# Moving a kernel's input transposes from TensorE to the DMA engines, with four PSUM buffers and a bf16 weight preparation

## The chip, the cores and the metric

The kernel runs on one core of one Trainium2 chip. The metric is device time in microseconds (us). Most repetitions of one kernel agree closely; a run that lies over 1.5% above the fastest of the same kernel is labelled slow. Comparisons below use fast runs, unless a sentence says otherwise. A ratio is the mean time of one kernel's fast runs over that of the kernel before in the same rounds on the same chip, so it is not quite the ratio of the medians quoted beside it.

Names: PE is TensorE (PEld its weight loads), ACT is ScalarE, DVE is VectorE, POOL is GpSimd, SP is SyncE (here it only issues DMAs). `L209` is line 209 of the kernel in question; each kernel has its own numbering.

## The reference

A gated recurrence over time feeds a "maximum of two projections" network. Four sequences of 6144 tokens have 256 features each; the hidden width is 1024.

```python
sig = 1 / (1 + exp(-f_logit))
f = lower_bound + (1 - lower_bound) * sig
h = f[:, t] * h + (1 - f[:, t]) * x[:, t]      # for every t; y[:, t] = h
g = maximum(y @ w1, y @ w2)
out = g @ w_out
```

Both kernels use max(a, b) = a + relu(b - a), so `out = relu(y @ (w2 - w1)) @ w_out + y @ (w1 @ w_out)`. In the code `w21` is w2 - w1, `wob` is w_out, and `w13b` is w1 @ w_out, computed once at the start.

## The kernel before

Work goes in 48 blocks of 512 tokens. The recurrence wants features on partitions and time along the row, but x and f arrive with tokens on partitions, so something has to transpose them. Here TensorE does, in bf16, after DMA loads that cast from fp32.

```python
TB, TSB, NSB = 512, 128, 4
ps_t = tile_pool(name="ps_t", bufs=2, PSUM)     # transposes: 2 banks
ps_d = tile_pool(name="ps_d", bufs=2, PSUM)     # dT: 2 banks
ps_o = tile_pool(name="ps_o", bufs=1, PSUM)     # psO0..psO3: 4 banks

def recurrence(j):
    for h in range(2):                          # two halves of the features
        for i in range(NSB):
            nc.tensor.transpose(tT[:, i*TSB:(i+1)*TSB], blk.xn[:, i, h*P:(h+1)*P], ident_b)
        for i in range(NSB):
            nc.tensor.transpose(tT[:, TB+i*TSB:TB+(i+1)*TSB], blk.fn[:, i, h*P:(h+1)*P], ident_b)
        nc.scalar.activation(out=u, in_=fT, func=AF.Sigmoid, scale=-1.0)
        # DVE: ff = 1 + (lb-1)*u ; v = (1-lb)*u*xT ; y = scan(ff, v)
        # ... cut ...

def moe(j):
    for fc in range(8):
        for kc in range(2):                     # dT = (y @ w21) transposed
            nc.tensor.matmul(dT, lhsT=w21[:, kc, fc*P:(fc+1)*P], rhs=yk[kc], ...)
        nc.scalar.activation(out=rt, in_=dT, func=AF.Relu)
    for fc in range(8):                         # 32 products of 256 columns
        for i in range(NSB):
            nc.tensor.matmul(psos[i], lhsT=rts[fc][:, i*TSB:(i+1)*TSB], rhs=wob[:, fc, :], ...)
    for i in range(NSB):                        # 8 products of 256 columns
        for kc in range(2):
            nc.tensor.matmul(psos[i], lhsT=yk[kc][:, i*TSB:(i+1)*TSB], rhs=w13b[:, kc, :], ...)
    # DVE copies psO to osb, SP stores osb
```

Of the kernel before, what the change touches and what calls it, by code (L numbers as in the profile page):

```python
# [9 lines left out]
FP32 = mybir.dt.float32  # L10
BF16 = mybir.dt.bfloat16
ALU = mybir.AluOpType
# [5 lines left out]
def kernel(  # L18
# [14 lines left out]
    assert D == 2 * P and DFF == 8 * P  # L33
    KC = D // P
    FC = DFF // P
    TB = 512
    TSB = 128
    NSB = TB // TSB
    assert S % TB == 0
    NBLK_PER_B = S // TB  # L40
    NBLK = B * NBLK_PER_B

    const = ctx.enter_context(tc.tile_pool(name="const", bufs=1))
    wpool = ctx.enter_context(tc.tile_pool(name="wpool", bufs=1))
    natpool = ctx.enter_context(tc.tile_pool(name="nat", bufs=3))
    midpool = ctx.enter_context(tc.tile_pool(name="mid", bufs=2))
    ypool = ctx.enter_context(tc.tile_pool(name="ypool", bufs=4))
    rpool = ctx.enter_context(tc.tile_pool(name="rpool", bufs=10))
    opool = ctx.enter_context(tc.tile_pool(name="opool", bufs=3))
    ps_t = ctx.enter_context(tc.tile_pool(name="ps_t", bufs=2, space=bass.MemoryType.PSUM))  # L50
    ps_d = ctx.enter_context(tc.tile_pool(name="ps_d", bufs=2, space=bass.MemoryType.PSUM))
    ps_o = ctx.enter_context(tc.tile_pool(name="ps_o", bufs=1, space=bass.MemoryType.PSUM))

    ident = const.tile([P, P], FP32)
    make_identity(nc, ident[:])
# [14 lines left out]
        op1=ALU.add,  # L70
    )

    w1n = wpool.tile([P, KC, DFF], FP32)
    nc.sync.dma_start(out=w1n[:], in_=moe_w1.rearrange("(kc p) f -> p kc f", p=P))
    w2n = wpool.tile([P, KC, DFF], FP32)
    nc.sync.dma_start(out=w2n[:], in_=moe_w2.rearrange("(kc p) f -> p kc f", p=P))
    w21 = wpool.tile([P, KC, DFF], BF16)
    nc.vector.tensor_tensor(out=w21[:], in0=w2n[:], in1=w1n[:], op=ALU.subtract)

    won = wpool.tile([P, FC, D], FP32)  # L80
    nc.sync.dma_start(out=won[:], in_=moe_w_out.rearrange("(fc p) c -> p fc c", p=P))
    wob = wpool.tile([P, FC, D], BF16)
    nc.vector.tensor_copy(out=wob[:], in_=won[:])

    w1T = wpool.tile([P, FC, D], FP32)
    for kc in range(KC):
        for g in range(FC // 4):
            pt = ps_d.tile([P, TB], FP32, name="dT")
            for j in range(4):
                fc = 4 * g + j  # L90
                nc.tensor.transpose(  # L91
                    pt[:, j * P : (j + 1) * P],
                    w1n[:, kc, fc * P : (fc + 1) * P],
                    ident[:],
                )
            for j in range(4):
                fc = 4 * g + j
                nc.scalar.copy(
                    out=w1T[:, fc, kc * P : (kc + 1) * P], in_=pt[:, j * P : (j + 1) * P]
                )  # L100

    w13b = wpool.tile([P, KC, D], BF16)
    for kc in range(KC):
        psw = ps_d.tile([P, TB], FP32, name="dT")
        for fc in range(FC):
            nc.tensor.matmul(  # L106
                psw[:, 0:D],
                lhsT=w1T[:, fc, kc * P : (kc + 1) * P],
                rhs=won[:, fc, :],
                start=(fc == 0),  # L110
                stop=(fc == FC - 1),
            )
        nc.scalar.copy(out=w13b[:, kc, :], in_=psw[:, 0:D])

    class Blk:
        pass

    blocks: list = []
    for b in range(B):
        for c in range(NBLK_PER_B):  # L120
            blk = Blk()
            blk.b = b
            blk.c = c
            blk.t0 = c * TB
            blocks.append(blk)

    def out_rows(blk, i0, n):
        r0 = blk.b * S + blk.t0 + i0 * TSB
        return out[r0 : r0 + n * TSB, :].rearrange("(i p) d -> p i d", p=P)

    ys = {}

    def load_nat(blk):
        xn = natpool.tile([P, NSB, D], BF16, name="xn")
        fn = natpool.tile([P, NSB, D], BF16, name="fn")
        nc.gpsimd.dma_start(  # L136
            out=xn[:],
            in_=x[blk.b, blk.t0 : blk.t0 + TB, :].rearrange("(i p) d -> p i d", p=P),
        )
        nc.gpsimd.dma_start(  # L140
            out=fn[:],
            in_=f_logit[blk.b, blk.t0 : blk.t0 + TB, :].rearrange(
                "(i p) d -> p i d", p=P
            ),
        )
        blk.xn = xn
        blk.fn = fn

    def recurrence(j):
        blk = blocks[j]  # L150
        prev = ys.get(j - 1) if blk.c > 0 else None
        yh = []
        for h in range(KC):
            tT = ps_t.tile([P, 2 * TB], BF16, name="tT")
            xT = tT[:, 0:TB]
            fT = tT[:, TB : 2 * TB]
            for i in range(NSB):
                nc.tensor.transpose(  # L158
                    tT[:, i * TSB : (i + 1) * TSB],
                    blk.xn[:, i, h * P : (h + 1) * P],  # L160
                    ident_b[:],
                )
            for i in range(NSB):
                nc.tensor.transpose(  # L164
                    tT[:, TB + i * TSB : TB + (i + 1) * TSB],
                    blk.fn[:, i, h * P : (h + 1) * P],
                    ident_b[:],
                )
            u = midpool.tile([P, TB], BF16, name="u")
            nc.scalar.activation(out=u[:], in_=fT, func=AF.Sigmoid, scale=-1.0)  # L170
            ff = midpool.tile([P, TB], BF16, name="ff")
            nc.vector.tensor_scalar(  # L172
                out=ff[:],
                in0=u[:],
                scalar1=lbm1[:, h : h + 1],
                scalar2=1.0,
                op0=ALU.mult,
                op1=ALU.add,
            )
            v = midpool.tile([P, TB], BF16, name="v")  # L180
            nc.vector.scalar_tensor_tensor(  # L181
                out=v[:],
                in0=u[:],
                scalar=om[:, h : h + 1],
                in1=xT,
                op0=ALU.mult,
                op1=ALU.mult,
            )
            y = ypool.tile([P, TB], BF16, name=f"y{h}")
            init = 0.0 if prev is None else prev[h][:, TB - 1 : TB]  # L190
            nc.vector.tensor_tensor_scan(  # L191
                out=y[:],
                data0=ff[:],
                data1=v[:],
                initial=init,
                op0=ALU.mult,
                op1=ALU.add,
            )
            yh.append(y)
        ys[j] = tuple(yh)  # L200

    def moe(j):
        blk = blocks[j]
        yk = ys[j]
        rts = []
        for fc in range(FC):
            dT = ps_d.tile([P, TB], FP32, name="dT")
            for kc in range(KC):
                nc.tensor.matmul(  # L209
                    dT[:, :],  # L210
                    lhsT=w21[:, kc, fc * P : (fc + 1) * P],
                    rhs=yk[kc][:, :],
                    start=(kc == 0),
                    stop=(kc == KC - 1),
                )
            rt = rpool.tile([P, TB], BF16, name="rt")
            nc.scalar.activation(out=rt[:], in_=dT[:], func=AF.Relu)  # L217
            rts.append(rt)
        psos = [ps_o.tile([P, D], FP32, name=f"psO{i}") for i in range(NSB)]
        for fc in range(FC):  # L220
            for i in range(NSB):
                nc.tensor.matmul(  # L222
                    psos[i][:, :],
                    lhsT=rts[fc][:, i * TSB : (i + 1) * TSB],
                    rhs=wob[:, fc, :],
                    start=(fc == 0),
                    stop=False,
                )
        for i in range(NSB):
            for kc in range(KC):  # L230
                nc.tensor.matmul(  # L231
                    psos[i][:, :],
                    lhsT=yk[kc][:, i * TSB : (i + 1) * TSB],
                    rhs=w13b[:, kc, :],
                    start=False,
                    stop=(kc == KC - 1),
                )
        for g in range(NSB // 2):
            osb = opool.tile([P, 2, D], FP32, name="osb")
            for q in range(2):  # L240
                nc.vector.tensor_copy(out=osb[:, q, :], in_=psos[2 * g + q][:, :])  # L241
            nc.sync.dma_start(out=out_rows(blk, 2 * g, 2), in_=osb[:])

    load_nat(blocks[0])
    if NBLK > 1:
        load_nat(blocks[1])
    recurrence(0)
    for j in range(NBLK):
        if j + 2 < NBLK:
            load_nat(blocks[j + 2])  # L250
        if j + 1 < NBLK:
            recurrence(j + 1)
        moe(j)


# [28 lines left out]
```

## Time and profile before

| | before |
|---|---|
| median, 16 runs | 501.34 us |
| span of the profiled run | 498.8 us |
| first `dT` matmul of the loop | 25.25 us |
| one block in the loop | 9.79 us |
| PE work in one block | 8.7 us |

The first view is the timeline of PE: start and duration in us, engine, line, operation, output<-inputs, shape, count, and in brackets the idle time before it with what ended it. This is one block of the kernel before.

```profile
201.27 0.39 PE L158 MATMUL tT<-ident_b,xn 128*128 128x128 bf16 x4
201.50 0.39 PE L164 MATMUL tT<-ident_b,fn 128*128 128x128 bf16 x4
...
202.38 0.81 PE L209 MATMUL dT<-y,w 128*128 128x512 bf16 x3
203.59 0.59 PE L209 MATMUL dT<-y,w 128*128 128x512 bf16 x2 [0.40 <-ACT rt L217]
204.03 0.27 PE L222 MATMUL psO<-wob,rt 128*128 128x256 bf16 x1
204.13 0.59 PE L209 MATMUL dT<-y,w 128*128 128x512 bf16 x2
...
206.81 0.59 PE L209 MATMUL dT<-y,w 128*128 128x512 bf16 x2
207.24 3.11 PE L222 MATMUL psO<-wob,rt 128*128 128x256 bf16 x27
210.19 1.04 PE L231 MATMUL psO<-w13b,y 128*128 128x256 bf16 x8
211.06 0.39 PE L158 MATMUL tT<-ident_b,xn 128*128 128x128 bf16 x4
```

Read the starts, not the durations: matmuls overlap, so durations add up to more than the time passed. The sixteen transposes take 0.89 us, and 40 `psO` products take 4.35 us at 108 ns each. The `dT` phase holds sixteen matmuls of 216 ns (3.45 us) and five early `psO` products (0.54 us), yet it lasts from 202.16 to 207.24 us: 1.1 us of it is waiting. (One `dT` record per block is missing in this trace, the one at 202.16; the trace of the changed kernel lacks one too, so it shows fifteen.) ScalarE's timeline for the same block shows what PE waits for:

```profile
201.97 1.08 ACT L170 ACTIVATE u<-tT 128x512 bf16<-128x512 bf16 x2 [3.66 <-DVE osb L241]
202.94 1.09 ACT L217 ACTIVATE rt<-dT 128x512 bf16<-128x512 f32 x2
204.28 1.14 ACT L217 ACTIVATE rt<-dT 128x512 bf16<-128x512 f32 x2 [0.25 <-PE dT L209]
```

Two sigmoids come first, then eight relus. With two `dT` buffers, PE can be only two tiles ahead of the relus. The page's DMA queues (packets, MB, share of 16 engines) of the kernel before; q0 carries the casting loads, q1 the stores and weights:

```profile
q0 software_dynamic: 50688, 25.17, 40.0%
q1 hardware_dynamic: 27968, 28.32, 17.7%
```

### The profile page before, as it was taken

The numbers are of one execution on the slowest core, as the hardware profiler recorded it, in microseconds if no ns is written. First come the engines' busy times: TensorE is split into PE (matmuls) and PEld (weight loads), VectorE is DVE, ScalarE is ACT, GpSimd is POOL, SyncE is SP. The second block draws the span as 40 slices with busy tenths as digits, with TensorE's granted clock in tenths as the row PEclk, the third lists the DMA queues.
The fourth block names the chain that finished last, engine by engine and source line by source line (L and its number), as shares of the span: only waits on it lengthen the run. The fifth ranks groups of instructions, "written<-read, shape, count | busy, mean of one in ns | idle before, by whom it ended". The sixth has DMA issues, their size and how long they took to land.

```text
span 498.8 us, 8901 instructions
## 1 busy us (share of the span) xinstructions
PE 450.9 (90%) x3456; PEld 314.3 (63%) x3504; DVE 295.3 (59%) x485; ACT 269.6 (54%) x500; POOL 72.2 (14%) x102
## 2 busy tenths in 40 slices
PE   2899999999999999999999999999999989999996
PEld 1765665676567656756765676667567656766663
DVE  2466467646765675566467656756664666567451
ACT  3266546645654665466456646654664566456543
POOL 4121112111111211121111112111211111120000
PEclk9999999999999999999999999999999999999999
DMA  8947546745664575467556645754674566464112
GB/s 246 175 87 122 90 87 131 121 85 107 124 111 85 127 116 97 85 131 119 90 103 126 111 85 127 115 98 85 132 121 86 107 119 113 86 125 88 44 43 84
DMA packets 78699, 54.06 MB, mean 108 GB/s; under 512 B 3393, under 2 KB 78145, under 8 KB 78657
## 3 DMA queue, kind: packets, MB, share of 16 engines
q0 software_dynamic: 50688, 25.17, 40.0%
q1 hardware_dynamic: 27968, 28.32, 17.7%
q8 instruction: 27, 0.44, 0.3%
q14 instruction: 16, 0.12, 0.1%
HBM read 53.48 MB, written 25.17 MB: 158 GB/s over the span
## 4 chain that ended last, share of the span: by engine, by line
PE 55%; ACT 26%; DVE 9%; issue 6%; DMA 2%; ACTq 0%; POOL 0%; DVEq 0%; POOLq 0%
PE psO L222 29%; PE dT L209 22%; ACT rt L217 16%; DVE osb L241 9%; ACT u L170 9%; DMA fn<-in_f_logit_dram 2%; PE psO L231 2%; PE dT L106 1%; PE dT L91 0%; ACTq L217 0%; PE tT L164 0%; POOL xn L136 0%; PE tT L158 0%; ACTq L170 0%; DVEq L279 0%
## 5 line engine op out<-in xcount | busy, mean ns | idle before, releaser
L217 ACT ACTIVATE rt<-dT 128x512 bf16<-128x512 f32 x384 | 216.4, 601 | 36.0 <-PE dT L209 35.0
L209 PE MATMUL dT<-y,w 128*128 128x512 bf16 x720 | 202.3, 377 | 32.0 <-ACT rt L217 20.5
L222 PE MATMUL psO<-wob,rt 128*128 128x256 bf16 x1536 | 214.4, 272 | 0.0
L222 PEld LDWEIGHTS <-rt 128*128 128x128 bf16 x1536 | 149.6, 97 | 53.6
L241 DVE COPY osb<-psO 128x256 f32<-128x256 f32 x192 | 68.2, 417 | 164.3 <-PE psO L231 164.3
L170 ACT ACTIVATE u<-tT 128x512 bf16<-128x512 bf16 x96 | 52.4, 595 | 172.7 <-DVE osb L241 164.7
L209 PEld LDWEIGHTS <-w 128*128 128x128 bf16 x768 | 72.3, 97 | 107.6 <-issue 59.9
L191 DVE TENSOR_TENSOR_SCAN y<-ff,y,v 128x512 bf16<-128x512 bf16 x88 | 112.5, 1278 | 1.5
L136 POOL DMA_DIRECT2D xn<-in_x_dram x48 | 35.7, 744 | 374.2 <-PE tT L164 364.6
L181 DVE SCALAR_TENSOR_TENSOR v<-u,om,tT 128x512 bf16<-128x512 bf16 x96 | 69.4, 723 | 0.0
L172 DVE TENSOR_SCALAR ff<-u,lbm 128x512 bf16<-128x512 bf16 x96 | 46.5, 485 | 20.5 <-ACT u L170 20.5
L231 PE MATMUL psO<-w13b,y 128*128 128x256 bf16 x384 | 49.8, 273 | 0.0
L231 PEld LDWEIGHTS <-y 128*128 128x128 bf16 x384 | 37.6, 98 | 4.3
L164 PE MATMUL tT<-ident_b,fn 128*128 128x128 bf16 x384 | 37.8, 221 | 2.4 <-DMA fn<-in_f_logit_dram 2.4
L158 PE MATMUL tT<-ident_b,xn 128*128 128x128 bf16 x384 | 37.6, 221 | 2.6 <-DMA xn<-in_x_dram 2.6
L140 POOL DMA_DIRECT2D fn<-in_f_logit_dram x48 | 36.3, 756 | 1.8 <-PE dT L209 1.3
L158 PEld LDWEIGHTS <-xn 128*128 128x128 bf16 x384 | 27.7, 99 | 4.2 <-DMA xn<-in_x_dram 3.0
L164 PEld LDWEIGHTS <-fn 128*128 128x128 bf16 x384 | 25.8, 99 | 2.8 <-DMA fn<-in_f_logit_dram 2.7
L91 PE MATMUL dT<-ident,w1n 128*128 128x128 f32 x16 | 4.1, 422 | 6.6 <-DMA w1n<-in_moe_w_dram 6.6
L191 DVE TENSOR_TENSOR_SCAN y<-ff,v 128x512 bf16<-128x512 bf16 x8 | 9.7, 1217 | 0.2
L106 PE MATMUL dT<-won,w1T 128*128 128x256 f32 x32 | 7.4, 390 | 0.0
L91 PEld LDWEIGHTS dT<-ident,w1n 128*128 128x128 f32 x16 | 3.1, 226 | 6.5 <-issue 6.5
(16 smaller groups left out, 18.1 us busy)
## 6 DMA issues: line engine op xcount, KB each, us to landing
out_dram<-osb SPq DMA_DIRECT2D x96, 256.0 KB, 2.3
xn<-in_x_dram POOLq DMA_DIRECT2D x48, 256.0 KB, 4.9
fn<-in_f_logit_dram POOLq DMA_DIRECT2D x48, 256.0 KB, 5.5
w1n<-in_moe_w_dram SPq DMA_DIRECT2D x1, 1024.0 KB, 5.2
w2n<-in_moe_w_dram SPq DMA_DIRECT2D x1, 1024.0 KB, 8.5
won<-in_moe_w_out_dram SPq DMA_DIRECT2D x1, 1024.0 KB, 14.1
lbc<-in_lower_bound_dram SPq DMA_DIRECT2D x1, 1.0 KB, 2.1
```

The costliest lines, as they stand in the source:

```text
L140: nc.gpsimd.dma_start(out=fn[:], in_=f_logit[blk.b, blk.t0 : blk.t0 + TB, :].rearrange("(i p) d -> p i d", p=P),)
L158: nc.tensor.transpose(tT[:, i * TSB : (i + 1) * TSB], blk.xn[:, i, h * P : (h + 1) * P], ident_b[:],)
L164: nc.tensor.transpose(tT[:, TB + i * TSB : TB + (i + 1) * TSB], blk.fn[:, i, h * P : (h + 1) * P], ident_b[:],)
L170: nc.scalar.activation(out=u[:], in_=fT, func=AF.Sigmoid, scale=-1.0)
L172: nc.vector.tensor_scalar(out=ff[:], in0=u[:], scalar1=lbm1[:, h : h + 1], scalar2=1.0, op0=ALU.mult, op1=ALU.add,)
L181: nc.vector.scalar_tensor_tensor(out=v[:], in0=u[:], scalar=om[:, h : h + 1], in1=xT, op0=ALU.mult, op1=ALU.mult,)
L191: nc.vector.tensor_tensor_scan(out=y[:], data0=ff[:], data1=v[:], initial=init, op0=ALU.mult, op1=ALU.add,)
L209: nc.tensor.matmul(dT[:, :], lhsT=w21[:, kc, fc * P : (fc + 1) * P], rhs=yk[kc][:, :], start=(kc == 0), stop=(kc == KC - 1),)
L217: nc.scalar.activation(out=rt[:], in_=dT[:], func=AF.Relu)
L222: nc.tensor.matmul(psos[i][:, :], lhsT=rts[fc][:, i * TSB : (i + 1) * TSB], rhs=wob[:, fc, :], start=(fc == 0), stop=False,)
L231: nc.tensor.matmul(psos[i][:, :], lhsT=yk[kc][:, i * TSB : (i + 1) * TSB], rhs=w13b[:, kc, :], start=False, stop=(kc == KC - 1),)
L241: nc.vector.tensor_copy(out=osb[:, q, :], in_=psos[2 * g + q][:, :])
```

## The change

The intent is to free PE of the transposes. x and f are first cast to bf16 into scratch memory in DRAM (a DRAM-to-DRAM DMA, in superblocks of 1024 tokens), and a transposing DMA then brings them to SBUF. The two PSUM banks of the transposes go to `dT`, which gets four buffers. The weight preparation runs in bf16, the `w13b` products come first, and four engines keep program order. The whole kernel also shows two smaller changes: eight output tiles (`osb`) instead of three, and the loads of w2 and w_out on ACT's queue instead of SP's. The core of the diff:

```diff
-    ps_t = ...tile_pool(name="ps_t", bufs=2, PSUM)
-    ps_d = ...tile_pool(name="ps_d", bufs=2, PSUM)
+    ps_d = ...tile_pool(name="ps_d", bufs=4, PSUM)
+    tpool = ...tile_pool(name="tpool", bufs=6)
+    RING = 3
+    xb = dram.tile([RING, SBT, D], BF16)          # SBT = 1024
+    fb = dram.tile([RING, SBT, D], BF16)
+    def cast_sb(s):
+        nc.gpsimd.dma_start(out=xb[s % RING, :, :], in_=x[b, t0 : t0 + SBT, :])
+        nc.gpsimd.dma_start(out=fb[s % RING, :, :], in_=f_logit[b, t0 : t0 + SBT, :])
+    def load_T(s):
+        for h in range(KC):
+            nc.sync.dma_start_transpose(out=xT[:], in_=xb[s % RING, :, h * P : (h + 1) * P])
+            nc.sync.dma_start_transpose(out=fT[:], in_=fb[s % RING, :, h * P : (h + 1) * P])
-            for i in range(NSB):
-                nc.tensor.transpose(...)           # 16 per block
...  # w1 transposes and w1 @ w_out in bf16; w13b products before the wob products
+    AHEAD = 2
+    with tc.manual_schedule(engines={SP, Pool, Activation, DVE}):
+        for s in range(min(AHEAD, NSBLK)):
+            cast_sb(s)
+        w21, wob, w13b = weight_prep()
+        for s in range(min(AHEAD, NSBLK)):
+            load_T(s)
+        rec(0)
+        cast_sb(AHEAD)
+        for s in range(NSBLK):
+            if s + AHEAD + 1 < NSBLK:
+                cast_sb(s + AHEAD + 1)
+            if s + AHEAD < NSBLK:
+                load_T(s + AHEAD)
+            for q in range(BLK_PER_SB):
+                ...                                # rec of the next block, then moe(s, q)
```

## The prediction

> **What bounds the kernel now.** TensorE paces it: PE is 90% busy on the profile page at a granted clock of 1.00 throughout. The timeline of PE shows one 512-token block every 9.79 us (output products at 200.40, 210.19 and 219.97 us); 48 blocks make 470 us, the rest is a start of 25.2 us (first `dT` matmul of the loop at 25.25 us) and a short tail. Inside a block (201.27 to 211.06 us):
>
> - 16 transposes (`tT`): 201.27 to about 202.16 us, so 0.89 us, 55 ns each.
> - 16 `dT` matmuls of 512 columns at 216 ns: 3.45 us.
> - 40 `psO` matmuls of 256 columns (32 with `wob`, 8 with `w13b`) at 108 ns: 4.35 us.
>
> That is 8.7 us; the other 1.1 us are stalls in the `dT` phase. `dT` has two buffers, ScalarE needs 0.57 us per relu against 0.43 us per `dT` tile, and the two sigmoids (1.08 us), which wait for the transposes, sit at the head of ScalarE's queue just before the relus. ScalarE then idles 3.66 us per block; DVE works 6.1 us.
>
> **What the change does.**
>
> 1. Takes the 16 transposes per block off PE: 0.89 us x 48 = 43 us, all on the chain.
> 2. Frees PSUM for four `dT` buffers, and lets the sigmoid run in ScalarE's idle time, because its input now comes from a DMA issued a superblock ahead. Four buffers cover the 0.14 us by which a relu is slower than a `dT` tile over eight tiles. About 50 us, on the chain.
> 3. Moves the `w13b` products first: neutral.
> 4. bf16 weight preparation: PE work at the start falls from 7.4 us (`w1T`, 32 matmuls) to about 3.5 us, but the first block now goes through cast to DRAM, transpose, sigmoid and scan in turn. I expect the loop to start near 27 us.
> 5. Adds DMA work. From the DMA queue view: casting loads took 40% of 16 engines for 25.2 MB written (126 GB/s if alone, 63 ns per 512 B packet), stores 17.7% for 25 MB of output and 3 MB of weights. Per 1024 tokens that is 8.3 us plus 3.3 us. The new transposes move 1 MB more. The Trainium skill ("DMA: Bandwidth & Descriptors", section "Latency and other measured facts") gives 261 GB/s for a transpose with a non-contiguous dimension; no trace here shows one. Estimate from that page: 4.0 us. Sum 15.6 us per 1024 tokens.
>
> **The sum.** PE-bound, a block takes 7.8 us: 27 + 48 x 7.8 + 5 = 406 us. But two blocks are 15.6 us, just what the DMA engines need, so the bound is uncertain. If the contiguous DRAM-to-DRAM cast is cheaper per byte, PE bounds; if the transposes reach only half the page's rate, the DMA needs 20 us per superblock and the time is near 500 us. I take a period of about 8.2 us per block: **426 us, range 402 to 482**. Chances: faster by over 2% 0.83, within 2% 0.06, slower 0.11.
>
> **What would show each step.** PE timeline: no `tT` matmuls, period 7.8 to 8.2 us. Waits: `dT` on ScalarE nearly gone (20.5 us before); the sigmoids fill ScalarE's idle gap. DMA share above 80% in the loop, against 58% to 60% before. If DMA bounds: sigmoids wait on `fT`, SP waits on the cast, PE has gaps of microseconds. Start: first loop matmul between 24 and 32 us.
>
> **What would make it wrong.** Transposes well below 261 GB/s, or slowed by the other traffic; a cast to DRAM slower than one to SBUF; stores stuck on SP behind transposes that wait for the cast until eight `osb` buffers run out; a PE order that puts `psO` matmuls before the copies that free their banks.

## The result, and the profile after

The changed kernel took 425.91 us (median of 11 runs, 421.08 to 435.46) against 501.34 us; the ratio of fast runs is 0.8456, 95% interval 0.8434 to 0.8478. The seven fast runs lie between 421.08 and 426.09 us, median 423.11. The profiled run was a slow one, with a span of 428.5 us. Five of the twelve runs are labelled slow; the 16 runs of the kernel before lie within 1.8 us of each other.

PE's timeline for one block of the changed kernel, then ScalarE's:

```profile
204.83 3.62 PE L206 MATMUL dT<-y,w 128*128 128x512 bf16 x15
208.28 1.04 PE L219 MATMUL psO<-w13b,y 128*128 128x256 bf16 x8
209.16 3.66 PE L228 MATMUL psO<-wob,rt 128*128 128x256 bf16 x32
212.65 3.62 PE L206 MATMUL dT<-y,w 128*128 128x512 bf16 x15
```

```profile
205.46 4.03 ACT L214 ACTIVATE rt<-dT 128x512 bf16<-128x512 f32 x8 [2.78 <-PE dT L206]
209.29 1.21 ACT L159 ACTIVATE u<-fT 128x512 bf16<-128x512 bf16 x2
```

The block takes 7.82 us (204.83 to 212.65), which is its PE work and nothing else. The relus run without a pause, and the sigmoids have moved behind them. Now the start. Here are the SP queue, DVE, ACT and PE around the beginning of the loop of the changed kernel:

```profile
9.61 11.59 SPq L142 DMA_TRANSPOSE xT<-xb  x1
21.25 3.54 SPq L146 DMA_TRANSPOSE fT<-fb  x1
...
24.63 2.29 DVE L95 TENSOR_TENSOR w<-w2n,w1n 128x2048 bf16<-128x2048 f32 x1 [19.56 <-DMA w1n<-in_moe_w_dram]
...
34.76 1.15 ACT L159 ACTIVATE u<-fT 128x512 bf16<-128x512 bf16 x2
...
37.74 1.86 PE L206 MATMUL dT<-y,w 128*128 128x512 bf16 x4 [4.71 <-DVE y L180]
```

The loop starts at 37.74 us, not at 25.25. DVE waits 19.56 us for w1, and the first transpose keeps the SP queue for 11.59 us. ACT keeps program order, so its first sigmoid stands behind the copies of the weight preparation, which need w1: from the arrival of w1 to the first `dT` matmul it is 13.1 us here, and 12.5 and 13.1 us in the runs `hold` and `deep` below. The transposes were not much earlier, though: POOL, which waits for the second `fT` of the first superblock, goes on only at 31.94 us. The DMA issues (KB each, us from issue to landing) of the kernel before, then of the changed one, show the weights landing late:

```profile
w1n<-in_moe_w_dram SPq DMA_DIRECT2D x1, 1024.0 KB, 5.2
won<-in_moe_w_out_dram SPq DMA_DIRECT2D x1, 1024.0 KB, 14.1
```

```profile
w1n<-in_moe_w_dram SPq DMA_DIRECT2D x1, 1024.0 KB, 23.3
won<-in_moe_w_out_dram ACTq DMA_DIRECT2D x1, 1024.0 KB, 26.1
```

A table of three pieces makes the balance. "Start" runs to the first long run of `wob` products, "loop" from there to the same point of the last block (47 periods), "rest" to the end. `w13last` and `deep` are experiments below; `w13last` has the changed kernel's work with another product order, and its profile is a fast one.

| profile (state) | start | loop | per block | rest | span |
|---|---|---|---|---|---|
| before (fast) | 30.2 | 460.4 | 9.80 | 8.2 | 498.8 |
| after (slow) | 44.5 | 375.8 | 8.00 | 8.2 | 428.5 |
| w13last (fast) | 43.1 | 369.7 | 7.87 | 8.8 | 421.6 |
| deep (fast) | 49.4 | 367.5 | 7.82 | 8.3 | 425.2 |

Between the two fast profiles of before and `w13last`, the loop gave 90.7 us and the start took 12.9 back. The slow profile of the changed kernel also holds one gap in the loop: 5.16 us of PE idle before 290 us, when a sigmoid waits for `fT`. For 5.1 us after it PE ran at a granted clock of 0.50, so the gap cost about 8 us in all (375.8 us of loop less the 367.5 of `deep`, which has no gap). The fast profile of `w13last` has only 0.89 us of idle there. The gap is therefore left out of the balance of fast runs, but the late transposes came with the change: no run of the kernel before was slow.

The DMA queues after (compare the two lines of before; q1 now carries the transposes too):

```profile
q1 hardware_dynamic: 128032, 51.40, 61.7%
q0 software_dynamic: 1536, 25.17, 34.6%
```

The cast's 25.17 MB now move in 1,536 packets of 16 KB instead of 50,688 of about 500 B, because both sides of the copy are contiguous (`pad` below breaks that up, and the packets number 49,920 again). And a warning on the share column, from windows of 100 us in the loop (busy us and counts by engine, granted clock, DMA share, GB/s), before and after:

```profile
100.00:200.00 100.00, 93.16 (x727) 64.83 (x736) 61.02 (x100) 54.77 (x100) 14.80 (x20) 1.00 0.59 106
```

```profile
100.00:200.00 100.00, 99.32 (x704) 69.97 (x715) 73.87 (x128) 64.10 (x128) 6.51 (x14) 1.00 1.07 204
```

The DMA share is 1.07, above one, while PE runs at its own pace. A share above one can only mean that packet times overlap, so a packet's time here is not all work. A share near one does not prove that the DMA engines set the pace; the experiments decide that.

### The profile page after: what moved, and what is told of

Read it like the earlier page. It is cut to its first block, busy times and chain, and to the rows that moved or that the text cites. A ratio compares the mean times of both kernels' runs of the same rounds, so it can differ in the third digit from the quotient of the medians.

```text
span 428.5 us, 7352 instructions
## 1 busy us (share of the span) xinstructions
PE 383.1 (89%) x2672; PEld 268.4 (63%) x2720; DVE 283.9 (66%) x486; ACT 249.6 (58%) x500; POOL 24.3 (6%) x54
## 3 DMA queue, kind: packets, MB, share of 16 engines
q0 software_dynamic: 1536, 25.17, 34.6%
## 4 chain that ended last, share of the span: by engine, by line
PE 83%; DMA 7%; SPq 7%; issue 2%; ACT 1%; DVE 0%; DVEq 0%; POOL 0%; ACTq 0%; POOLq 0%
PE psO L228 37%; PE dT L206 36%; PE psO L219 10%; DMA fT<-fb 5%; SPq L142 4%; SPq L146 2%; DMA xb<-in_x_dram 2%; ACT rt L214 1%; DVE osb L238 0%; ACT u L159 0%; DVEq L284 0%; POOL ident masks.py:197 0%; ACTq L159 0%; POOLq masks.py:199 0%; ACTq L214 0%
## 5 line engine op out<-in xcount | busy, mean ns | idle before, releaser
L214 ACT ACTIVATE rt<-dT 128x512 bf16<-128x512 f32 x384 | 194.0, 624 | 127.2 <-PE dT L206 126.8
L206 PE MATMUL dT<-y,w 128*128 128x512 bf16 x720 | 175.4, 385 | 12.6 <-ACT rt L214 5.2
L228 PE MATMUL psO<-wob,rt 128*128 128x256 bf16 x1536 | 175.6, 273 | 0.0
L206 PEld LDWEIGHTS <-w 128*128 128x128 bf16 x768 | 75.9, 99 | 92.8 <-issue 14.6
L170 DVE SCALAR_TENSOR_TENSOR v<-u,om,xT 128x512 bf16<-128x512 bf16 x96 | 71.5, 745 | 0.0
L159 ACT ACTIVATE u<-fT 128x512 bf16<-128x512 bf16 x96 | 58.1, 684 | 15.3 <-DMA fT<-fb 13.2
L161 DVE TENSOR_SCALAR ff<-u,lbm 128x512 bf16<-128x512 bf16 x96 | 32.4, 337 | 9.0 <-ACT u L159 9.0
L82 POOL DMA_DIRECT2D xb<-in_x_dram x24 | 11.9, 497 | 312.0 <-DMA xT<-xb 311.6
L85 POOL DMA_DIRECT2D fb<-in_f_logit_dram x24 | 11.8, 492 | 14.1 <-DMA fT<-fb 12.0
L125 PE MATMUL dT<-wob,w1T 128*128 128x256 bf16 x16 | 3.1, 379 | 0.0
## 6 DMA issues: line engine op xcount, KB each, us to landing
w1n<-in_moe_w_dram SPq DMA_DIRECT2D x1, 1024.0 KB, 23.3
```

The costliest lines, as they stand in the source:

```text
L82: nc.gpsimd.dma_start(out=xb[s % RING, :, :], in_=x[b, t0 : t0 + SBT, :])
L85: nc.gpsimd.dma_start(out=fb[s % RING, :, :], in_=f_logit[b, t0 : t0 + SBT, :])
L159: nc.scalar.activation(out=u[:], in_=fT[:, c], func=AF.Sigmoid, scale=-1.0)
L161: nc.vector.tensor_scalar(out=ff[:], in0=u[:], scalar1=lbm1[:, h : h + 1], scalar2=1.0, op0=ALU.mult, op1=ALU.add,)
L170: nc.vector.scalar_tensor_tensor(out=v[:], in0=u[:], scalar=om[:, h : h + 1], in1=xT[:, c], op0=ALU.mult, op1=ALU.mult,)
L206: nc.tensor.matmul(dT[:, :], lhsT=w21[:, kc, fc * P : (fc + 1) * P], rhs=yk[kc], start=(kc == 0), stop=(kc == KC - 1),)
```

## The experiments

Ten kernels ran. All gave the right output except `alone`.

**b4: only the buffers, transposes still on PE.** In the kernel before, each of the four psO tiles (256 columns) takes a bank, though a bank holds the 512 columns of a `dT` tile. Packing them in pairs frees two banks. The order of products changes with it, so two things differ from the kernel before: the 128-token groups now run one after the other.

```diff
-    ps_d bufs=2
+    ps_d bufs=4
-        psos = [ps_o.tile([P, D], FP32, name=f"psO{i}") for i in range(NSB)]
-        for fc in range(FC): for i in range(NSB): ...wob...; for i in range(NSB): ...w13b...
+        pso2 = [ps_o.tile([P, 2, D], FP32, name=f"psO{g}") for g in range(NSB // 2)]
+        psos = [pso2[i // 2][:, i % 2, :] for i in range(NSB)]
+        for i in range(NSB): (for fc in range(FC): ...wob...), then ...w13b...
```

> The kernel before, transposes still on TensorE, but with four dT buffers: the four psO tiles are packed two to a bank (their products then run one 128-token group after the other), which frees two banks. If the 1.1 us of stall per block came from the two dT buffers, the period falls from 9.79 to about 8.8 us and the time to about 453 us. If the stall came from the sigmoids standing behind the transposes in ScalarE's queue, four buffers do not cure it and the time stays above 480 us.

Measured: 481.71 us, ratio 0.9611. By the number that is the second branch, buffers do not cure it. PE's timeline tells another story:

```profile
208.24 3.62 PE L209 MATMUL dT<-y,w 128*128 128x512 bf16 x16
211.69 1.69 PE L223 MATMUL psO<-wob,rt 128*128 128x256 bf16 x9
213.22 0.38 PE L231 MATMUL psO<-w13b,y 128*128 128x256 bf16 x2
```

The `dT` phase is down to 3.45 us, so its stall is gone. But nine products of 108 ns (0.97 us) now take 1.53 us: the first token group needs all eight relus, and the last one ends at 213.05 us. The order that the packing forced had brought in a new wait of about 0.56 us per block. That wanted a second try.

**b4x: the buffers alone, in an order that does not wait.** Two passes, groups 0 and 2, then 1 and 3, which lie in different banks.

```diff
-        for i in range(NSB):
-            for fc in range(FC): ...wob...
-            ...w13b...
+        for half in ((0, 2), (1, 3)):
+            for fc in range(FC):
+                for i in half: ...wob...
+            for i in half: ...w13b...
```

> As b4, but the psO products run in two passes of two 128-token groups each, so that the last relu of a block is needed about 0.9 us later. In b4 the period was 9.27 us and TensorE waited about 0.6 us per block for that last relu, a side effect of the packing. If the whole 1.1 us of stall came from two dT buffers, the period is now 8.7 us and the time about 453 us; if sigmoids behind the transposes keep a part of it, it stays at 9.0 to 9.3 us, 468 to 482 us.

Measured: 456.42 us, ratio 0.9108.

```profile
207.37 3.62 PE L209 MATMUL dT<-y,w 128*128 128x512 bf16 x16
210.82 1.91 PE L224 MATMUL psO<-wob,rt 128*128 128x256 bf16 x16
...
216.08 3.62 PE L209 MATMUL dT<-y,w 128*128 128x512 bf16 x16
```

The period is 8.71 us, the PE work of a block with transposes. The whole 1.1 us of stall goes with two more buffers, although the sigmoids still stand between the transposes and the relus. The order of the `psO` products differs here too; the next run changes the buffer count and nothing else.

**psd2: the changed kernel with two `dT` buffers.**

```diff
-    ps_d = ...tile_pool(name="ps_d", bufs=4, PSUM)
+    ps_d = ...tile_pool(name="ps_d", bufs=2, PSUM)
```

> The changed kernel with two dT buffers in place of four. If the sigmoids' place on the chain was the stall, it stays cured: period about 7.8 us, time within 5 us of the changed kernel. If the buffer count matters by itself, TensorE waits again on the relus, which take 0.50 us each against 0.43 us per dT tile: 0.3 to 0.9 us more per block, 440 to 468 us.

Measured: 458.28 us, ratio 0.9157.

```profile
207.01 1.03 PE L206 MATMUL dT<-y,w 128*128 128x512 bf16 x4
...
215.53 1.03 PE L206 MATMUL dT<-y,w 128*128 128x512 bf16 x4
```

The period is 8.52 us, so 0.70 us of stall per block return. The rest of the change had cured only about 0.4 us of the 1.1 (9.79 less 0.89 for the transposes less 8.52); whether by the sigmoids moved off the chain or by the `w13b` products that now fill waits of PE, no run tells apart. The buffer count is what matters, and with four buffers the sigmoids' place no longer does.

**addback: give PE its lost work again.** Each `dT` matmul gets a dummy of 128 columns ahead of it, whose result is overwritten.

```diff
             for kc in range(KC):
+                nc.tensor.matmul(dT[:, 0:TSB], lhsT=w21[:, kc, ...], rhs=yk[kc][:, 0:TSB],
+                                 start=True, stop=True)
+            for kc in range(KC):
                 nc.tensor.matmul(dT[:, :], ...)
```

> The changed kernel with sixteen more matmuls of 128 columns per block on TensorE (their results are overwritten, the output stays right), as many and as wide as the transposes that the change took away. If TensorE bounds the loop, 0.89 us x 48 = 43 us come back: about 466 us, or some 8 us less because DMA then has more room and the long gap near 285 us disappears. If DMA bounds the loop, less than 20 us come back.

Measured: 466.19 us, ratio 0.931: 43 us above the fast runs of the changed kernel (423.11).

```profile
200.42 0.28 PE L206 MATMUL dT<-y,w 128*128 128x128 bf16 x2
...
209.14 0.28 PE L206 MATMUL dT<-y,w 128*128 128x128 bf16 x2
```

The period is 8.72 us, 0.90 more. So PE sets the loop's pace, and taking the transposes away was worth their full PE time.

**hold: casts wait for the weights.** One tiny POOL copy that reads `wob` stands before the second cast.

```diff
-        for s in range(min(AHEAD, NSBLK)):
-            cast_sb(s)
+        cast_sb(0)
         w21, wob, w13b = weight_prep()
+        hold = const.tile([P, 1], BF16)
+        nc.gpsimd.tensor_copy(out=hold[:], in_=wob[:, 0, 0:1])
+        cast_sb(1)
```

> The changed kernel, but the casts of superblocks 1 and 2 wait until w_out has landed. If the loop starts late (first dT matmul at 37.7 us) because the casts issued ahead crowd out the weights (w1 and w_out landed 23 and 26 us after issue), the weights land by about 12 us, the first dT matmul of the loop comes near 25 us and the time falls to about 412 us. If the latency of the chain cast, transpose, sigmoid, scan sets the start, the first dT matmul stays later than 32 us and the time stays above 420 us.

Measured: 423.42 us, ratio 0.8421. The first half of the expectation held roughly (w1 was there at 14.75 us and not by 12), the second did not. Lines of PE:

```profile
27.29 1.87 PE L206 MATMUL dT<-y,w 128*128 128x512 bf16 x4 [4.71 <-DVE y L180]
...
44.52 3.57 PE L206 MATMUL dT<-y,w 128*128 128x512 bf16 x8 [5.42 <-ACT rt L214]
...
65.68 3.57 PE L206 MATMUL dT<-y,w 128*128 128x512 bf16 x8 [3.34 <-ACT rt L214]
```

The loop starts 10.4 us earlier, then PE stands still twice, 8.8 us in all, while sigmoids wait for `fT`. After each wait the granted clock was 0.50, and the eight `dT` matmuls took 3.4 us instead of 1.7. The gain was lost to a new wait: the casts that were held back were also the lookahead.

**deep: three superblocks of lookahead.**

```diff
-    AHEAD = 2     # RING = 3, tpool bufs=6
+    AHEAD = 3     # RING = 4, tpool bufs=8
```

> The changed kernel with one more superblock of lookahead (three ahead, ring of four, eight transposed tiles). If the gap of 5 to 7 us in the middle of the run and the spread of 421 to 435 us come from single late transposes that two superblocks of lookahead do not cover, the gaps go, the time is near 418 us and the spread below 5 us. If the DMA engines as a whole are too slow, deeper lookahead only moves the gaps and the time stays at 423 to 430 us.

Measured: 427.51 us (426.99 to 428.61), ratio 0.854. The gaps and the spread went, as the first theory says (loop 367.5 us, exactly 47 x 7.82), but the total did not fall to 418. (For the spread the chip is not excluded as a reason: `pad`, with the shorter lookahead, ran on the same chip and spread by only 0.7 us.)

```profile
42.73 1.87 PE L206 MATMUL dT<-y,w 128*128 128x512 bf16 x4 [4.71 <-DVE y L180]
```

The fourth superblock cast at the start pushed the loop back by another 5.0 us. Casts of 1, 3 and 4 superblocks issued beside the weights, in the first 6 us, give a first `dT` matmul at 27.3, 37.7 and 42.7 us: about 5 us for each.

**pad: casts in small pieces.** Scratch rows of 272 instead of 256 elements keep the cast from running contiguously.

```diff
-    xb = dram.tile([RING, SBT, D], BF16)
+    xb = dram.tile([RING, SBT, D + 16], BF16)      # fb likewise; only [0:D] is used
```

> The changed kernel with rows of the DRAM scratch padded from 256 to 272 elements, so that the cast cannot run in long contiguous pieces and moves in rows of 512 B, as it did before the change. If the large cast packets (1,536 in all, 16 KB each) are what holds up the weights and the transposes, w1 lands in under 12 us instead of 23 and the loop starts before 32 us; the cast's own share of the DMA engines rises from 34.6% to about 45%. If only the number of bytes counts, the weights land as late as before and the total gets longer, 430 us or more.

Measured: 421.89 us (421.63 to 422.33), ratio 0.8421. DVE waits for w1 until 10.84 us instead of 24.63:

```profile
10.84 2.29 DVE L95 TENSOR_TENSOR w<-w2n,w1n 128x2048 bf16<-128x2048 f32 x1 [5.73 <-DMA w1n<-in_moe_w_dram]
```

The byte count is the same and the cast takes more of the DMA engines (46.9%), yet the weights land 13.8 us sooner. So it was the cast in large packets that held them up. This agrees with the Trainium skill, "DMA: Bandwidth & Descriptors", section "Queues, rings and completion order": each engine goes round the queues with work and drains a whole packet of one before it turns to the next. No run here shows these turns themselves, and the padded cast is also slower (the first transpose can be issued at 15.52 us instead of 9.61), which may have helped the weights. The loop itself starts at 32.00 us and not before: with the weights there in time, the first sigmoid waits until 29.01 us for `fT`, whose transposes share the engines with three superblocks of casts.

```profile
32.00 1.87 PE L206 MATMUL dT<-y,w 128*128 128x512 bf16 x4 [12.38 <-DVE y L180]
...
43.20 3.66 PE L228 MATMUL psO<-wob,rt 128*128 128x256 bf16 x32
```

Even this start gains next to nothing: the later sigmoids of the first blocks wait for `fT` as well, and the long run of `wob` products begins at 43.20 us, against 44.47 in the changed kernel and 43.06 in `w13last`. The weights are early here, but the transposes, behind a slower cast, are as late as the weights were.

**alone: the DMA work by itself.** No matmuls: eight superblocks cast, then transposed in reverse order (so that the first transpose waits for the last casts), then the whole output stored. One profiled run, of unknown state.

> Wrong output on purpose: the DMA work by itself, one kind after the other, no matmuls. Eight superblocks are cast to DRAM, then all are transposed into SBUF, then the whole output is stored. If the transpose rate of 261 GB/s holds, the 8.4 MB of transposes take 32 us; if the share of the queues in the changed kernel is right (about 180 us for 25 MB, 140 GB/s), 60 us. The casts should take 50 us (6.2 us per superblock) by that kernel's queue shares, 66 us by those of the kernel before.

(The 261 GB/s are the figure of the Trainium skill that the prediction cites, from "DMA: Bandwidth & Descriptors", section "Latency and other measured facts".)

The SP queue's timeline:

```profile
40.72 2.30 SPq L142 DMA_TRANSPOSE xT<-xb  x1
...
82.51 1.30 SPq L142 DMA_TRANSPOSE xT<-xb  x1
83.85 1.30 SPq L146 DMA_TRANSPOSE fT<-fb  x1
...
87.74 72.76 SPq L251 DMA_DIRECT2D out_dram<-osb  x96
```

| per superblock of 1024 tokens | predicted | alone |
|---|---|---|
| casts, 2 MB read, 1 MB written | 8.3 us | 4.9 us (from 1.3 to 40.7 us for eight) |
| transposes, 1 MB | 4.0 us | 5.4 us (four at 1.34 us; 196 GB/s) |
| stores, 1 MB | 3.3 us | 3.0 us (96 in 72.76 us) |
| sum | 15.6 us | 13.3 us |

Two blocks on PE take 15.64 us, so by these figures, measured one kind at a time, the DMA engines have some 15% of room. Part of the fall in the casts is the measure: 8.3 us was a queue's share of the engines in a busy kernel. By the same measure the casts take 6.2 us in the changed kernel (34.6% of 428.5 us over 24 superblocks) and 8.2 us in `pad`. Whether 196 GB/s is the engines' pace or that of SP, which needs 1.30 us to issue each transpose, this run does not tell. Both expectations missed the casts (50 or 66 us; they took 39), and the transposes fell between the two figures (47 us from first issue to last landing).

**w13last: the old order of products.**

```diff
-        for i in range(NSB): for kc in range(KC): ...w13b (start)...
         for fc in range(FC): for i in range(NSB): ...wob...
+        for i in range(NSB): for kc in range(KC): ...w13b (stop)...
```

> The changed kernel with the eight w13b products of a block after the wob products again, as before the change. The prediction called this order neutral: the time stays within 3 us of the changed kernel (421 to 435 us by runs so far, so within its spread). If the order helps TensorE to bridge the wait for the relus, the period rises above 7.82 us, by up to 0.3 us per block, and the time to 430 to 440 us.

Measured: 424.31 us, ratio 0.8454; the period is 7.82 us. The order is neutral.

**hybrid: the old way for the first two superblocks.** PE has nothing to do at the start, so superblocks 0 and 1 come by casting loads to SBUF and transposes on PE, into `dT` buffers; the casts to DRAM wait until `wob` is there; the lookahead is three.

```diff
+    HB = 2
     def rec(j):
-            xT, fT = xfT[s, h]
+            xT, fT = pe_T(j, h) if s < HB else xfT[s, h]
...
+        for j in range(HB * BLK_PER_SB):
+            load_nat(j)                             # casting loads, 512 tokens each
         w21, wob, w13b = weight_prep()
+        nc.gpsimd.tensor_copy(out=hold[:], in_=wob[:, 0, 0:1])
+        for s in range(HB, AHEAD + 1):
+            cast_sb(s)
```

> The changed kernel with lookahead of three superblocks, but superblocks 0 and 1 take the old way (casting loads to SBUF, transposes on TensorE, into two of the four dT buffers), and the casts to DRAM for superblocks 2 and 3 wait until w_out has landed. TensorE idles at the start anyway, so its 3.6 us of transposes are nearly free. If the late start (37.7 us) is the whole of what the changed kernel lost, the loop starts near 25 us, no gap follows, and the time is 25 + 48 x 7.82 + 4 + 5, about 409 us. If the DMA engines have too little room to build up the lookahead later on, as in the run that held the casts back, gaps of 5 us each come between 40 and 90 us and the time stays above 416 us.

Measured: 412.62 us (411.18 to 413.35), ratio 0.8222. It beats both kernels.

```profile
24.15 0.39 PE L234 MATMUL dT<-y,w 128*128 128x512 bf16 x1 [2.95 <-DVE y L208]
...
27.97 4.78 PE L234 MATMUL dT<-y,w 128*128 128x512 bf16 x12
32.58 3.66 PE L256 MATMUL psO<-wob,rt 128*128 128x256 bf16 x32
```

The `wob` products start at 32.6 us against 43.1 in `w13last`, and no later wait in PE's timeline is longer than 0.24 us. This kernel combines three changes (the transposes on PE, the held casts, the deeper lookahead), which were not run one by one. The few us missing to 409 are in the first block: its twelve `dT` matmuls at 27.97 us run at about 0.39 us each instead of 0.216. That is in line with the Trainium skill, "TensorE: Matmul & The Clock Gate", section "Part 1: The HAM clock gate": an idle TensorE falls to half its clock and needs a stretch of work to leave it. The profile of this run shows it too: the granted clock was 0.56 from 27.97 to 32.58 us and 1.00 in the block after.

## Why the prediction was right or wrong

The time was right (426 us predicted; 425.91 median of all runs, 423.11 of the fast ones). The mechanism of the loop was right too, but that the total agrees so closely is luck: two terms missed in opposite directions.

- *"TensorE paces it", 8.7 us of work and 1.1 us of stall.* Right: b4x removes the stall alone and runs at 8.71 us.
- *"0.89 us x 48 = 43 us, all on the chain".* Right: addback costs 43 us.
- *"Four buffers ... About 50 us, on the chain."* Right: b4x brings the period from 9.79 to 8.71 us, 52 us over 48 blocks. Its time fell by only 45 us, since its own loop starts later (first `wob` products at 35.4 us against 27.1). The supporting cause, the sigmoids at the head of the queue, was a smaller part: about 0.4 us at most with two buffers (`psd2`), nothing with four (`b4x`).
- *"`w13b` products first: neutral."* Right (w13last).
- *"I expect the loop to start near 27 us."* Wrong: 37.74 us. This step forgot that three superblocks of casts are issued beside the weights, in the first 4.7 us. The prediction counted the latency of the chain and not its competitors; `hold` and `deep` show the competition, about 5 us for each superblock cast early. `pad` shows that w1 is late only with the large packets, and that with small ones the transposes are as late and the `wob` products begin no sooner.
- *The DMA sum of 15.6 us.* Too high: 13.3 us by parts. It sized the casts by the old packets (63 ns for each 512 B), but a contiguous copy moves in 16 KB pieces; it took 6.2 us by the same measure and 4.9 us alone, instead of 8.3. It sized the transposes from the skill's page at 4.0 us; they took 5.4.
- *"a period of about 8.2 us per block"* Wrong: 7.82. It was an allowance for a DMA limit that the sum of parts does not show. Over 48 blocks the allowance is 18 us. The late start took 10.7 of them. The first block's slow ramp (5.9 us from its first `dT` matmul to its `wob` products instead of 3.45, at a granted clock of 0.63) and stray gaps in the loop (369.7 less 367.5 us) took about 4.7 in the fast profile of `w13last`, and the fast runs' median lies 2.9 us below the prediction. So the errors cancelled, by luck.
- *"DMA share above 80%"* came true (1.07), and means less than the prediction gave it: the loop was still PE's.

What stays open: why transposes come late near 285 us in some runs of the changed kernel and hardly in others (one slow run was profiled), and what limits a lone stream of transposes.

## What to carry to other kernels

When an engine waits on the drain of its PSUM tiles, price the buffers separately from the work that a change takes away: here two more banks alone brought 1.08 of the 1.97 us that each block gained (`b4x`), with no transposing DMA. The shares depend on the order of counting: added last, after the rest of the change, the two banks are worth 0.70 us (`psd2`). Work issued ahead competes with what the first block needs, so plan the start as a stage of its own: use the idle engine there, and hold back bulk transfers until the weights are in, but build up the lookahead right after. Count DMA cost by the packets that a copy will really use, since making both sides contiguous took a quarter off the cast's share of the engines (8.3 to 6.2 us per superblock) and at the same time made it a worse neighbour for the weights.

## What the Trainium skill lacked or had wrong

- "DMA: Bandwidth & Descriptors", "Latency and other measured facts", gives 261 GB/s for a transpose with a non-contiguous dimension, and "Advanced Engine Details and Errata", "X-Bar Transpose (TRN2)", says that transposing DMAs are as fast as plain ones. A lone stream of [1024 x 128] bf16 transposes ran at 196 GB/s, while the stores of the same run reached 346 GB/s (256 KB in 0.758 us). It is open whether issuing limits it.
- No page gives SP's time to issue a transpose of this size on this chip (the DMA page has only a cycle count for small tiles, in a comparison of generations): 1.30 us alone, and up to 11.59 us in the changed kernel, with the casts in flight.
- No page gives the cost of a casting DRAM-to-DRAM copy: 2.43 us for 1 MB read and 0.5 MB written when both sides are contiguous (16 KB per packet in the profile).
- The rule on draining whole packets is in "DMA: Bandwidth & Descriptors", but not what it costs a neighbour: with 16 KB packets 1 MB of weights landed after 23.3 us, with 512 B packets after 9.5 us.
- "Perfetto Trace Analysis", "Identifying the Most-Contended Engine", already says that occupancy misleads for the DMA engines. That their share can pass 1 while another engine sets the pace (1.07 in this loop) is not there.
